# Threshold attention and an exact-gelu MLP in fp32: the first queries and keys loaded in longer rows, and the weights' conversion spread over ScalarE, GpSimd and SyncE

## The chip, the cores and the metric

The kernel runs on one core of a Trainium2 chip. A core has TensorE (PE) for matmuls, VectorE (DVE), ScalarE (ACT) and GpSimd (POOL) for elementwise work, SyncE (SP), which here only issues transfers, and 16 DMA engines. Operands lie in SBUF with 128 partitions, and matmuls write to PSUM. Each engine takes its instructions in the order of the program; engines wait for one another by semaphores. The metric is the device time of one execution in microseconds (us).

## The reference

```python
# q, k, v: (8 batches, 8 heads, 576 rows, 64);  tau = 0.02
scores = (1 / sqrt(64)) * q @ k.T
thresh = max(scores, axis=-1) - tau
scores = where(scores >= thresh, scores, -1e9)
attn = exp(scores - max(scores))
attn = attn / (sum(attn) + 1e-9)
x = (attn @ v), heads side by side        # (4608, 512)
h = x @ w_in                              # w_in (512, 2048)
g = 0.5 * h * (1 + erf(h / sqrt(2)))
out = g @ w_out                           # w_out (2048, 512)
```

The weights w_in and w_out reach the kernel as 64-bit floats. It converts them to 32 bits on the chip.

## The kernel before

**Work units.** Two heads of one batch form a pair; there are 32 pairs (NP), four to a batch (HP). The 576 query rows of a pair are cut in five chunks: four of 128 rows for each head and one in which the 64 last rows of both heads are joined (chunk NC = 4). One pair and one chunk make a slot. In a slot TensorE computes the scores (L348), VectorE their negated maxima (nmx, L360), GpSimd the threshold (thr, L361), ScalarE the exp (L363), and VectorE masks the exp by the threshold and sums it (L379).

**Order of slots.** The four pairs of the first batch are called early (EARLY = 4). Slots 0 to 7 take chunks 0 and 1 of these pairs, slots 8 to 19 chunks 2, 3 and 4; from slot 20 on (BATCH) pairs come one by one with all their chunks. All instructions are written out in program order in one loop over slots (n), and nothing reorders them. So an engine that waits keeps everything behind that instruction waiting.

**Early pairs.** Their q and k are loaded by `load_early` with a row of the sequence on a partition, and turned on TensorE by `turn_qk_early` (L265, tails L273), with ScalarE copying the result to SBUF. Keys may be in any order, so k's rows are taken four to a partition, in rows of 256 bytes of memory each per head; v's early load uses the same order. The masked exp is turned on TensorE against a diagonal matrix that holds the reciprocal of the sums: GpSimd adds 1e-9 to the sums (den, L382), VectorE takes the reciprocal (L390), ScalarE makes the diagonals (diag, L393), and a slot later `turn_p_early` turns (L291) and ScalarE copies to pT (L299, L302, L309, L314). `weigh_v` multiplies pT by v (xT, L465), and ScalarE copies the product to x (L470). For later pairs VectorE and DMAs turn p, and the division comes at the end, on GpSimd (L484).

**Weights.** There are 32 pieces of 128 x 512, 16 of w_in and then 16 of w_out. `load_piece` loads the raw 8-byte words of one piece (raw, L146) and, from three bytes further on, the same words again (shifted, L148): 1 MB for a piece. Four pieces can be in flight; even ones lie in two x tiles and odd ones in the two halves of turned_p. The first two are issued by SyncE before the loop; all others are issued by GpSimd, one of them whenever a piece has been converted. The generator `conversions` emits a piece's steps: VectorE masks the exponent (power, L168), ScalarE rebiases it (L169), VectorE takes the mantissa's bits (L174), puts the sign on the power (L176) and multiplies mantissa and power (L178). L168 of the next piece goes ahead of L174 of this one. `convert` emits steps in each slot until a budget in ns (the sum of the `yield` values) is used up: 0 in slot 0, 3400 in slots 1 to 7, 3650 in slots 8 to 18 and all that is left in slot 19. The call stands behind the masked sum of its slot and ahead of `diagonal`, so VectorE takes the reciprocal after the conversion of that slot.

**MLP.** A block is 256 tokens. `block_steps` yields its matmuls one at a time (hT, L536, then o_ps, L550), and `fill` places them between the slots' other work, when a piece that they need has been converted earlier in program order. From slot 20 on, `gelus_held` runs the first gelus, whose inputs were kept so that ScalarE needn't change its function table earlier, and `table` changes the table back. The last blocks are multiplied in `strassen` (L670), after all slots.

**Transfers.** SyncE issues the early loads, in the order of the program: q, k and v of pairs 0 to 3 (k of pair 0 by ScalarE, k of pair 1 by GpSimd) ahead of the slots that use them, then q, k and v of pairs 4 and 5 (`load`, L214 and L223), at the last chunks of pairs 1 and 2. GpSimd issues those of later pairs.

Of the kernel before, what the change touches and what calls it, by code (L numbers as in the profile page):

```python
# [8 lines left out]
FP32 = mybir.dt.float32  # L9
# [9 lines left out]
def kernel(  # L19
# [33 lines left out]
    P = 128  # L53
# [72 lines left out]
    loaded = [0]  # L126
    converted = [0]

    def load_piece(eng=nc.gpsimd):
        if loaded[0] == len(pieces):  # L130
            return
        dst, src = pieces[loaded[0]]
        loaded[0] += 1
        if not wide:
            nc.sync.dma_start(dst, src)
            converted[0] += 1
            load_piece()
            return
        k = loaded[0] - 1
        if k % 2:  # L140

            room = pd[k // 2 % 2].bitcast(U32)
            raw, shifted = room[:, 0:2 * PIECE], room[:, 2 * PIECE:4 * PIECE]
        else:
            raw, shifted = (xg.tile([P, 2 * PIECE], U32, tag="x", name=s) for s in ("raw", "shifted"))
        eng.dma_start(raw, src.bitcast(U32))  # L146
        n = 8 * PIECE - 4
        eng.dma_start(shifted.bitcast(U8)[:, 0:n], src.bitcast(U8)[:, 3:3 + n])  # L148
        raws.append((dst, raw, shifted))

    def conversions():

        vec = nc.vector
        ahead = None  # L160
        while raws or ahead:
            piece = None
            if raws:
                dst, raw, shifted = raws.pop(0)
                hi = raw.rearrange("p (f w) -> p f w", w=2)[:, :, 1]
                top = shifted.rearrange("p (f w) -> p f w", w=2)[:, :, 0]
                power = gp.tile([P, PIECE], U32, tag="g", name="power")
                vec.tensor_scalar(power, hi, 0x7FF00000, None, op0=ALU.bitwise_and)  # L168
                nc.scalar.activation(power, power, AF.Relu, bias=rebias, scale=8.0)  # L169
                piece = dst, hi, top, dst.bitcast(U32), power  # L170
                yield 340
            if ahead:
                dst, hi, top, mant, power = ahead
                vec.tensor_scalar(mant, top, 0x0FFFFFFF, 0x10000000, op0=ALU.bitwise_and, op1=ALU.bitwise_or)  # L174
                yield 340
                vec.scalar_tensor_tensor(power, hi, 0x80000000, power, op0=ALU.bitwise_and, op1=ALU.bitwise_or)  # L176
                yield 720
                vec.scalar_tensor_tensor(dst, mant, 2.0 ** -28, power.bitcast(FP32), op0=ALU.mult, op1=ALU.mult)  # L178
                load_piece()
                converted[0] += 1  # L180
                yield 700
            ahead = piece

    conv = {"steps": None, "debt": 0.0}
# [1 line left out]
    def convert(ns):  # L186

        if conv["steps"] is None:
            conv["steps"] = conversions()
        conv["debt"] += ns  # L190
        while conv["debt"] > 0:
            took = next(conv["steps"], None)
            if took is None:
                return
            conv["debt"] -= took
# [31 lines left out]
    def load_early(p):  # L227
        b, hp = divmod(p, HP)
        s = st[p] = {}
        for name, src in (("q", q), ("k", k)):  # L230
            t = s[name] = ld.tile([P, NC + 1, P], FP32, tag=name, name=name)
            eng = (nc.scalar, nc.gpsimd)[p] if p < 2 and name == "k" else nc.sync
            for e in range(2):
                order = "(t p) d -> p t d" if name == "q" else "(p t) d -> p t d"
                eng.dma_start(
                    t[:, 0:NC, e * D:(e + 1) * D], src[b, 2 * hp + e, 0:MAIN, :].rearrange(order, p=P))
            eng.dma_start(
                t[0:TAIL, NC, :].rearrange("p (e d) -> p e d", e=2),
                src[b, 2 * hp:2 * hp + 2, MAIN:S, :].rearrange("e s d -> s e d"),
            )  # L240

    def load_v_early(p):
        b, hp = divmod(p, HP)
# [5 lines left out]
    def turn_qk_early(p):  # L249


        s = st[p]
        if 2 <= p < HP:
            qT = op.tile([P, MAIN], FP32, tag="o_sb", name="qT")
            kT = pd_tail[p - 2].rearrange("p b i -> p (b i)")
        else:
            qT = ld.tile([P, MAIN], FP32, tag="qT", name="qT")
            kT = ld.tile([P, TAIL + S], FP32, tag="kT", name="kT")
        s["qT"], s["kT"] = qT, kT
        qt = s["q_tail"] = q_tail[p % 4]  # L260
        for name in "qk":
            t = s[name]
            tr = ps.tile([P, NC, P], FP32, tag="mm", name="tr")
            for c in range(NC):
                nc.tensor.transpose(tr[:, c, :], t[:, c, :], ident)  # L265
            src = tr.rearrange("p c s -> p (c s)")
            if name == "q":
                nc.scalar.activation(qT, src, AF.Copy, bias=0.0, scale=q_scale)
            else:
                nc.scalar.copy(kT[:, TAIL:S], src)  # L270
        tr = ps.tile([P, NC, P], FP32, tag="mm", name="tr")
        for j, name in enumerate("qk"):
            nc.tensor.transpose(tr[:, j, 0:TAIL], s.pop(name)[0:TAIL, NC, :], ident[0:TAIL, 0:TAIL])  # L273
        nc.scalar.copy(kT[:, S:S + TAIL], tr[:, 1, 0:TAIL])
        nc.scalar.copy(kT[D:P, 0:TAIL], tr[D:P, 1, 0:TAIL])
        for e in range(2):
            rows = slice(e * D, (e + 1) * D)
            nc.scalar.activation(
                qt[rows, e * TAIL:(e + 1) * TAIL], tr[rows, 0, 0:TAIL], AF.Copy, bias=0.0, scale=q_scale[rows])

    def turn_p_early(p, i):


        s = st[p]
        if i == 0 or (p < HP and i == 2):
            s["pT"] = [one.tile([P, KR, S], FP32, tag=f"pT{e}", name=f"pT{e}") for e in range(2)]
        w, diag = s.pop(("p", i)), s.pop(("diag", i))
        n = 1 if i == NC else 2

        def turn(to, cols, e):  # L290
            nc.tensor.matmul(to, lhsT=w[:, cols], rhs=diag[:, e, :], start=True, stop=True)  # L291

        for e in range(n):
            tr = ps.tile([P, NC, P], FP32, tag="mm", name="tr")
            for c in range(NC):
                at = e * (S + TAIL) + c * P
                turn(tr[:, c, :], slice(at, at + P), e)
            if i < NC:
                nc.scalar.copy(s["pT"][e][:, 0:NC, i * P:(i + 1) * P], tr)  # L299
        if i == NC:  # L300
            for e in range(2):
                nc.scalar.copy(s["pT"][e][:, 0:NC, MAIN:S], tr[:, :, e * TAIL:(e + 1) * TAIL])  # L302
        tails = s["pT"][0][:, NC, :]
        tr = ps.tile([P, NC, P], FP32, tag="mm", name="tr")
        if i < NC:
            for e in range(2):
                at = MAIN + e * TAIL
                turn(tr[e * TAIL:(e + 1) * TAIL, 0, :], slice(at, at + TAIL), e)
            nc.scalar.copy(tails[:, i * P:(i + 1) * P], tr[:, 0, :])  # L309
            return  # L310
        turn(tr[0:TAIL, 0, :], slice(MAIN, S), 0)
        for e in range(2):
            rows = slice(e * TAIL, (e + 1) * TAIL)
            nc.scalar.copy(tails[rows, MAIN:S], tr[0:TAIL, 0, rows])  # L314

    def scale_q(p):
        t = st[p]["q"]
# [132 lines left out]
    def weigh_v(p, lo, hi):  # L450


        b, hp = divmod(p, HP)
        s = st[p]
        xT = ps.tile([P, 512], FP32, tag="mm", name="xT")
        for c in range(KR):
            for e in range(2):
                f = slice(e * D, (e + 1) * D)
                to = xT[f, 0:hi - lo]
                if p < EARLY:  # L460
                    rhs = s["pT"][0 if c == NC else e][:, c, lo:hi]
                else:
                    to = to.rearrange("p (g s) -> p g s", s=2 * Q)
                    rhs = by_64(s["pT"][e])[:, lo // (2 * Q):hi // (2 * Q), c, :]
                nc.tensor.matmul(  # L465
                    to, lhsT=s["v"][:, e, c, :], rhs=rhs, start=(c == 0), stop=(c == KR - 1))
        for n, o, at, size in in_blocks(b, lo, hi):
            if n not in x_blk:
                x_blk[n] = xg.tile([P, N_DM, TOK], FP32, tag="x", name="x")
            nc.scalar.copy(x_blk[n][:, hp, o:o + size], xT[:, at - lo:at - lo + size])  # L470

    def in_blocks(b, lo, hi):
        while lo < hi:
# [311 lines left out]
    for t in q_tail + v_sb:  # L785
        nc.gpsimd.memset(t, 0.0)
    for _ in range(2):
        load_piece(nc.sync)
    turn_qk_early(0)
    load_v_early(0)  # L790
    load_early(2)
# [31 lines left out]
    for n in range(len(slots) + WEIGH + 1):  # L823
# [60 lines left out]
            scale_q(p + 1)  # L884
        if p >= HP - 1 and i == 2 and p + 1 < NP:
            turn_qk(p + 1)
        convert(0 if n == 0 else 3400 if n < 2 * HP else 3650 if n < BATCH - 1 else 1e9)
        if early:
            diagonal(p, i)
        if not early:  # L890
# [51 lines left out]
```

## Time and profile before

Three runs took 1392.73, 1394.04 and 1394.57 us. The profiled execution spans 1393.5 us.

| what | value |
|---|---|
| TensorE busy | 1360.1 us, 98% |
| VectorE busy | 891.4 us, 64% |
| ScalarE busy | 640.4 us, 46% |
| GpSimd busy | 433.4 us, 31% |
| VectorE's conversion, 10 to 150 us: L168, L174, L176, L178 | 435, 415, 684, 691 ns each |
| ScalarE's rebias L169 | 724 ns each |
| GpSimd's issue of one raw load | 0.55 to 0.6 us |
| SyncE's issue of one raw load | 0.35 to 0.43 us |

In groups of instructions a name left of the arrow is what is written, one to the right what is read. "Idle before" is time in which the engine had nothing running ahead of that instruction, and the name behind it is what the engine then waited for. A line with "SPq" or "POOLq" shows the issue of a transfer by SyncE or GpSimd, not its length. The granted clock is TensorE's, as a share of its full speed.

### The profile page before, as it was taken

What the parts mean: (1) busy time and instruction counts of PE and PEld (TensorE: products, weight loads), DVE (VectorE), ACT (ScalarE), POOL (GpSimd) and SP (SyncE); (2) the same over time, 40 slices, a digit from 0 to 9 for tenths busy, and PEclk for the clock granted to TensorE, in tenths of its full rate; (3) what the DMA queues carried; (4) which work ended last, traced back from release to release, by engine and by line L of the source; (5) the groups of instructions that cost most, each with busy time, mean ns of one, the idle gap of its engine ahead of it and who ended that gap; (6) DMA issues with size and microseconds to landing.
All of it is one profiled execution on the core that took longest, in us unless ns stands there. A gap on an engine that the chain in (4) does not pass through costs nothing.

```text
span 1393.5 us, 19980 instructions
## 1 busy us (share of the span) xinstructions
PE 1360.1 (98%) x6608; PEld 967.6 (69%) x6608; DVE 891.4 (64%) x1734; ACT 640.4 (46%) x1165; POOL 433.4 (31%) x895
## 2 busy tenths in 40 slices
PE   6799899999999999999999999999999999999999
PEld 4577547557457467466466476588888888888887
DVE  5889687788888888888888888764132242241330
ACT  5666636547447457457457357241141240330420
POOL 4444254455455455555554551100000000000000
PEclk9899999999999999999999999999999999999999
DMA  9889267667777777777778776500000001001000
GB/s 271 251 299 287 52 132 168 145 151 160 176 164 169 168 181 179 163 190 184 159 192 187 152 178 141 118 1 8 23 1 23 23 1 46 16 0 53 9 8 23
DMA packets 219557, 169.18 MB, mean 121 GB/s; under 512 B 121456, under 2 KB 203952, under 8 KB 219456
## 3 DMA queue, kind: packets, MB, share of 16 engines
q1 hardware_dynamic: 194768, 112.84, 36.2%
q0 software_dynamic: 23488, 54.77, 12.9%
q8 instruction: 54, 0.88, 0.3%
q10 hardware_dynamic: 1200, 0.30, 0.1%
q14 instruction: 47, 0.39, 0.1%
HBM read 72.73 MB, written 12.52 MB: 61 GB/s over the span
## 4 chain that ended last, share of the span: by engine, by line
PE 88%; DVE 5%; DMA 3%; ACT 3%; issue 1%; SPq 0%; POOL 0%; ACTq 0%; DVEq 0%
PE bank L670 35%; PE o_ps L550 16%; PE hT L536 14%; PE sc L348 12%; PE xT L465 10%; DVE p L379 1%; DVE power L176 1%; ACT p L363 1%; DMA k<-in_k_dram 1%; ACT diag L393 1%; DVE power L168 1%; DVE w_in L178 1%; DMA turned_p<-in_moe_w_in_dram 1%; DMA turned_p<-in_moe_w_out_dram 1%; DVE w_out L178 1%
## 5 line engine op out<-in xcount | busy, mean ns | idle before, releaser
L363 ACT ACTIVATE p<-sc,nmx 128x576 f32<-128x576 f32 x288 | 201.9, 738 | 271.5 <-DVE nmx L360 271.5
L379 DVE SCALAR_TENSOR_TENSOR p<-sc,thr,p 128x576 f32<-128x576 f32 x288 | 225.4, 816 | 70.0 <-ACT p L363 68.9
L360 DVE TENSOR_REDUCE nmx<-sc 128x1 f32<-128x576 f32 x288 | 205.3, 750 | 69.4 <-PE sc L348 68.6
L536 PE MATMUL hT<-x,w_in 128*128 128x256 f32 x1024 | 241.1, 385 | 0.0
L550 PE MATMUL o_ps<-w_out,g 128*128 128x512 f32 x512 | 237.3, 604 | 2.1 <-ACT pT L302 2.1
L536 PEld LDWEIGHTS hT<-x,w_in 128*128 128x128 f32 x1024 | 189.5, 190 | 49.2 <-issue 23.5
L361 POOL TENSOR_SCALAR thr<-nmx,tau_eff 128x1 f32<-128x1 f32 x288 | 84.4, 293 | 395.9 <-DVE nmx L360 395.1
L550 PEld LDWEIGHTS o_ps<-w_out,g 128*128 128x128 f32 x512 | 92.9, 189 | 112.7 <-issue 108.6
L465 PE MATMUL xT<-pT,v 128*64 128x256 f32 (+1 forms) x1280 | 163.9, 409 | 0.6 <-issue 0.6
L348 PE MATMUL sc<-kT,qT 64*128 64x288 f32 x960 | 158.5, 433 | 3.4 <-DVE p L379 2.5
L426 DVE STREAM_TRANSPOSE turned_p<-p 128x1152 f32<-128x1152 f32 x112 | 154.4, 1378 | 3.9
L348 PEld LDWEIGHTS sc<-kT,qT 64*128 64x128 f32 x960 | 90.3, 188 | 77.2 <-issue 64.8
L465 PEld LDWEIGHTS xT<-pT,v 128*64 128x64 f32 x1280 | 89.0, 137 | 73.2 <-issue 13.9
L670 PE MATMUL bank<-x,w_in 128*128 128x256 f32 x480 | 116.7, 379 | 0.0
L670 PE MATMUL bank<-w_out,unit 128*128 128x256 f32 x520 | 115.5, 379 | 0.0
L223 POOL DMA_DIRECT2D v<-in_v_dram x208 | 111.1, 537 | 4.6 <-issue 2.6
L670 PEld LDWEIGHTS bank<-w_out,unit 128*128 128x128 f32 x520 | 98.8, 190 | 13.4
L670 PEld LDWEIGHTS bank<-x,w_in 128*128 128x128 f32 x480 | 91.2, 190 | 12.8 <-issue 0.5
L670 PE MATMUL bank<-v,unit 128*128 128x256 f32 x320 | 82.1, 379 | 0.0
L214 POOL DMA_DIRECT2D q<-in_q_dram x104 | 70.9, 687 | 10.0 <-issue 9.1
L670 PE MATMUL bank<-unit,turned_p 128*128 128x256 f32 x320 | 73.1, 379 | 0.0
L509 ACT ACT_TABLE_LOAD x56 | 71.8, 1283 | 1.0
(154 smaller groups left out, 1487.6 us busy)
## 6 DMA issues: line engine op xcount, KB each, us to landing
pT<-turned_p SPq DMA_DIRECT2D x448, 160.0 KB, 3.7
pT<-pd_tail SPq DMA_DIRECT2D x112, 80.0 KB, 3.1
q<-in_q_dram POOLq DMA_DIRECT2D x104, 72.0 KB, 3.4
k<-in_k_dram POOLq DMA_DIRECT2D x104, 72.0 KB, 3.0
inv<-turned SPq DMA_DIRECT2D x56, 128.0 KB, 4.0
v<-in_v_dram POOLq DMA_DIRECT2D x156, 40.0 KB, 3.2
x<-x SPq DMA_DIRECT2D x10, 512.0 KB, 4.8
raw<-in_moe_w_out_dram POOLq DMA_DIRECT2D x8, 512.0 KB, 5.4
```

Of the source, the lines that this page charges most:

```text
L223: eng.dma_start(t[r:P:4, e, 0:n, :], rows[:, r * KR:r * KR + n, :])
L348: nc.tensor.matmul(sc[e][:, h, 0:HALF], lhsT=lhsT, rhs=s["kT"][rows, at:at + HALF], start=True, stop=True)
L360: nc.vector.tensor_reduce(nmx[:, e:e + 1], sc, axis=AXIS.XY, op=ALU.max, negate=True)
L361: nc.gpsimd.tensor_scalar(thr[:, e:e + 1], nmx[:, e:e + 1], -1.0, tau_eff, op0=ALU.mult, op1=ALU.subtract)
L363: nc.scalar.activation(w[:, e * S:(e + 1) * S].rearrange("p (h s) -> p h s", h=2), sc, AF.Exp, bias=nmx[:, e:e + 1], scale=1.0)
L379: nc.vector.scalar_tensor_tensor(row, sc[e][:, :, 0:HALF], thr[:, e:e + 1], row, op0=ALU.is_ge, op1=ALU.mult, accum_out=den[e])
L426: nc.vector.transpose(turned_p[:, :, i // 2, 0:NB, i % 2 * Q:(i % 2 + 1) * Q], w.rearrange("p (e b i) -> p e b i", e=2, i=Q))
L465: nc.tensor.matmul(to, lhsT=s["v"][:, e, c, :], rhs=rhs, start=(c == 0), stop=(c == KR - 1))
L509: nc.scalar.activation(t, src, AF.Gelu)
L536: nc.tensor.matmul(hT[:, j % 2, :], lhsT=w_in_sb[c][:, j * P:(j + 1) * P], rhs=x_blk[n][:, c, :], start=(c == 0), stop=(c == N_DM - 1))
L550: nc.tensor.matmul(o[:, 0:d_model], lhsT=g[j][:, m * P:(m + 1) * P], rhs=w_out_sb[j], start=(j == 0), stop=(j == N_DF - 1))
L670: nc.tensor.matmul(to, lhsT=l, rhs=r, start=start and k == 0, stop=k == len(pairs) - 1, skip_group_check=not start)
```

## The change

Four edits go together.

1. Early q and k are laid out with the head ahead of the chunk, so that a partition takes rows that lie next to each other in memory: two rows of q (512 bytes) and four of k (1 KB) at a time. Each turn of 128 columns becomes two matmuls of 64 columns, one for each head. The rows of q then come in another order within 256 tokens, which `weigh_v` puts right as it copies to x.
2. The product of mantissa and power leaves VectorE: ScalarE makes the mantissa a float and scales it, and GpSimd multiplies it by the power. `load_piece` for the piece four further on is now called after L176. The budgets of `convert` are 2000 in slots 1 and 2 and 2600 up to slot 18.
3. SyncE issues all raw weights.
4. For the last early pair (p = 3), VectorE copies the turned tails of p in place of ScalarE. This happens in slot 20.

```diff
-    def load_piece(eng=nc.gpsimd):
+    def load_piece(eng=nc.sync):
...
                 vec.scalar_tensor_tensor(power, hi, 0x80000000, power, op0=ALU.bitwise_and, op1=ALU.bitwise_or)
+                load_piece()
+                nc.scalar.activation(dst, mant, AF.Copy, bias=0.0, scale=2.0 ** -28)
+                nc.gpsimd.tensor_tensor(dst, dst, power.bitcast(FP32), op=ALU.mult)
+                converted[0] += 1
                 yield 720
-                vec.scalar_tensor_tensor(dst, mant, 2.0 ** -28, power.bitcast(FP32), op0=ALU.mult, op1=ALU.mult)
-                load_piece()
-                converted[0] += 1
-                yield 700
...
-            t = s[name] = ld.tile([P, NC + 1, P], FP32, tag=name, name=name)
+            t = s[name] = ld.tile([P, 2, NC + 1, D], FP32, tag=name, name=name)
...
+                rows = src[b, 2 * hp + e, 0:MAIN, :]
+                if name == "q":
+                    eng.dma_start(t[:, e, 0:NC, :].rearrange("p (g c) d -> p g (c d)", c=2),
+                                  rows.rearrange("(g p c) d -> p g (c d)", p=P, c=2))
+                else:
+                    eng.dma_start(t[:, e, 0:NC, :], rows.rearrange("(p t) d -> p t d", p=P))
...
-                nc.tensor.transpose(tr[:, c, :], t[:, c, :], ident)
+                for e in range(2):
+                    nc.tensor.matmul(tr[e * D:(e + 1) * D, c, :], lhsT=t[:, e, c, :], rhs=ident, start=True, stop=True)
...
+            copy = nc.vector.tensor_copy if p == EARLY - 1 else nc.scalar.copy
             for e in range(2):
-                nc.scalar.copy(s["pT"][e][:, 0:NC, MAIN:S], tr[:, :, e * TAIL:(e + 1) * TAIL])
+                copy(s["pT"][e][:, 0:NC, MAIN:S], tr[:, :, e * TAIL:(e + 1) * TAIL])
...
-        convert(0 if n == 0 else 3400 if n < 2 * HP else 3650 if n < BATCH - 1 else 1e9)
+        convert(0 if n == 0 else 2000 if n < 3 else 2600 if n < BATCH - 1 else 1e9)
```

More of the change, by code (lines that the diff above doesn't have):

```diff
@@ L230, in load_early @@
         for name, src in (("q", q), ("k", k)):
-            t = s[name] = ld.tile([P, NC + 1, P], FP32, tag=name, name=name)
+            t = s[name] = ld.tile([P, 2, NC + 1, D], FP32, tag=name, name=name)
             eng = (nc.scalar, nc.gpsimd)[p] if p < 2 and name == "k" else nc.sync
             for e in range(2):
[L234 to L240, printed above, removed]
+                rows = src[b, 2 * hp + e, 0:MAIN, :]
[4 more added lines that the diff above has]
+                    eng.dma_start(t[:, e, 0:NC, :], rows.rearrange("(p t) d -> p t d", p=P))
+            eng.dma_start(t[0:TAIL, :, NC, :], src[b, 2 * hp:2 * hp + 2, MAIN:S, :].rearrange("e s d -> s e d"))
     def load_v_early(p):
@@ L272, in turn_qk_early @@
         for j, name in enumerate("qk"):
-            nc.tensor.transpose(tr[:, j, 0:TAIL], s.pop(name)[0:TAIL, NC, :], ident[0:TAIL, 0:TAIL])
+            t = s.pop(name)
+            for e in range(2):
+                nc.tensor.matmul(tr[e * D:(e + 1) * D, j, 0:TAIL], lhsT=t[0:TAIL, e, NC, :],
+                                 rhs=ident[0:TAIL, 0:TAIL], start=True, stop=True)
         nc.scalar.copy(kT[:, S:S + TAIL], tr[:, 1, 0:TAIL])
@@ L313, in turn_p_early @@
             rows = slice(e * TAIL, (e + 1) * TAIL)
-            nc.scalar.copy(tails[rows, MAIN:S], tr[0:TAIL, 0, rows])
+            copy(tails[rows, MAIN:S], tr[0:TAIL, 0, rows])
     def scale_q(p):
@@ L469, in weigh_v @@
                 x_blk[n] = xg.tile([P, N_DM, TOK], FP32, tag="x", name="x")
-            nc.scalar.copy(x_blk[n][:, hp, o:o + size], xT[:, at - lo:at - lo + size])
+            to, x = x_blk[n][:, hp, o:o + size], xT[:, at - lo:at - lo + size]
+            if p < EARLY and size == TOK:
+                to = to.rearrange("q (p c) -> q c p", c=2)
+                x = x.rearrange("q (c p) -> q c p", c=2)
+            nc.scalar.copy(to, x)
     def in_blocks(b, lo, hi):
@@ L787 @@
     for _ in range(2):
-        load_piece(nc.sync)
+        load_piece()
     turn_qk_early(0)
```

## The prediction

> **What bounds the kernel now.** I read first which engine is busy in which stretch of the trace, because a change that touches only the first 32 weight pieces can move only the stretch in which they are converted. Columns: stretch, its length, busy us of TensorE (PE), its weight loads, VectorE (DVE), ScalarE (ACT), GpSimd (POOL), granted clock, DMA share, GB/s.
>
> ```profile
> 8.00:82.00 74.00, 59.42 (x381) 45.65 (x382) 58.97 (x129) 50.22 (x108) 30.76 (x62) 0.88 0.93 279
> 82.00:150.00 68.00, 64.98 (x401) 49.00 (x399) 60.33 (x133) 44.43 (x97) 27.95 (x56) 1.00 0.75 250
> 150.00:175.00 25.00, 21.03 (x88) 11.52 (x88) 12.23 (x21) 16.13 (x28) 7.29 (x20) 0.93 0.29 62
> 175.00:900.00 725.00, 724.26 (x3486) 433.53 (x3484) 607.38 (x1085) 400.15 (x608) 359.66 (x738) 1.00 0.73 165
> 900.00:1393.00 493.00, 487.85 (x2248) 426.22 (x2246) 151.71 (x362) 127.14 (x323) 1.69 (x3) 1.00 0.05 18
> ```
>
> After 175 us TensorE is busy 724 of 725 us and then 488 of 493; the change removes no TensorE work there, so nothing is to be had. Before it, TensorE idles 14.6 + 3.0 + 4.0 us, and its clock is 0.88 up to 82 us. So at stake are some 20 us at the start. The table of waits to 175 us says what TensorE waits for, and one line what the conversion waits for:
>
> ```profile
> PEld tr L291 <- ACT diag L393: 18.9, 10, 3.5
> ...
> PE tr L291 <- ACT diag L393: 14.4, 6, 3.1
> ...
> DVE power L168 <- DMA raw<-in_moe_w_in_dram: 4.6, 1, 4.6
> ...
> PE o_ps L550 <- ACT pT L302: 2.1, 1, 2.1
> ```
>
> The diag of a slot follows the reciprocal of its denominators (L390), which stands on VectorE behind that slot's conversion. VectorE is thus the bound up to 82 us: the reciprocals end at 14.27 us (slot 0), 21.81, 32.62, 40.13 and, for slot 9, 82.23. Slots 10 to 19 end at 149.53, 6.73 us each. VectorE's groups from 10 to 150 us (busy us, mean ns) give the conversion's price:
>
> ```profile
> L178 DVE SCALAR_TENSOR_TENSOR w_in<-w_in,power 128x512 f32<-128x512 uint32 x16 | 11.1, 691 | 0.4
> L178 DVE SCALAR_TENSOR_TENSOR w_out<-w_out,power 128x512 f32<-128x512 uint32 x16 | 11.1, 691 | 0.4
> L176 DVE SCALAR_TENSOR_TENSOR power<-raw,power 128x512 uint32<-128x512 uint32 x16 | 10.9, 684 | 0.1
> ```
>
> **What the Trainium skill says.** (1) "SBUF — State Buffer", section "Who interferes with whom": VectorE and GpSimd share a port pair under an exclusive lock; a VectorE operation with two SBUF inputs, or in a 2-port mode, and a GpSimd operation that reads SBUF block each other, while a tensor_reduce doesn't contend. The trace agrees as far as it goes: GpSimd's small add on the denominators (L382) takes 0.24 us at 14 us, and 0.62 and 0.89 us at 18 and 25 us, where conversion operations run on VectorE. (2) "GPSIMD Engine Reference", section "3.1 Elementwise — side-by-side cycle accounting": about 2.6 cycles an element on GpSimd, against 1 on VectorE. The trace's own slope serves instead (below). (3) "DMA: Bandwidth & Descriptors", section "Issuing engines are not separate DMA queues": all issuers use the same 16 DMA engines, another issuer saves only its own issue time. No run here shows it yet. (4) "TensorE: Matmul & The Clock Gate", section "What's actually happening": after an idle window of about 3.4 us the clock is halved until it is busy as long. The trace agrees: 20 turns (L291) take 2.42 us, and 3.9 to 4.4 us after idle.
>
> **The change part by part.**
> *VectorE loses L178.* 32 times; back to back they stand 0.61 us apart, so 32 × 0.61 = 19.6 us of VectorE's time. A slot with two pieces has about 3.2 us of softmax and 3.3 us of conversion. It falls to about 5.4; I take 5.7, since diag and exp on ScalarE now queue behind the new activations.
> *ScalarE gains 32 activations* of 128x512. The rebias (L169) of that shape takes 724 ns: 32 × 0.72 = 23 us. With 50.2 busy of 74 us and 44.4 of 68 there is room, so it costs only the 0.2 to 0.3 us a slot just named.
> *GpSimd gains 32 multiplies.* Its two-input multiply (L484) takes 729 ns for 256 columns and 457 for 128: 2.1 ns a column, so 729 + 256 × 2.1 = 1.27 us for 512, in all 41 us. It loses 60 issues of raw weights (L146, L148, 0.55 to 0.6 us each: 34 us). Its busy time hardly moves. Who waits? The threshold (L361) behind a multiply, which is needed only after the exp; and VectorE, if the lock holds it. Bounds of the lock: nothing, to one multiply of 1.2 us per slot where two pieces follow each other. I take nothing for the sum and keep the other end.
> *SyncE gains those 60 issues* (0.35 to 0.43 us each there), but in its own order. Before, GpSimd issued piece 2 at 14.29 us and VectorE took it up at 20.54. Now it stands behind SyncE's 28 loads of early q, k and v, which run from 10.78 to 32.40 us:
>
> ```profile
> 31.28 0.61 SPq L246 DMA_DIRECT2D v<-in_v_dram  x1
> 31.93 0.47 SPq L247 DMA_DIRECT2D v<-in_v_dram  x1
> 32.50 7.68 SPq L214 DMA_DIRECT2D q<-in_q_dram  x4
> ```
>
> Their waits are 2 us and more in places and shrink with the shorter lists of rows, so I take 28 us (bounds 24 and 32). Plus 4.6 us to land: 32.6. VectorE, in order, waits at slot 1's third L168 from 20.5 on: 12 us, and slot 1's reciprocal, its diag and the turns on TensorE stand behind it. The 4.6 us wait for piece 4 (28 to 32 us) goes: +7.5 us. Later the 16 loads of pair 4 (L214, L223: 11 to 20 us of SyncE) stand ahead of pieces 25 to 30, and those of pair 5 ahead of 31: up to 3 us in slots 14 to 17; I take 2.
> *Rows of 512 bytes and 1 KB.* Instead of 8192 rows of 256 bytes, 2048 of 512 and 1024 of 1 KB; the first q and k come somewhat sooner. In exchange each turn of 128 columns becomes two matmuls of 64. 16 turns take 4.0 us for q, 3.1 for k. The two halves use different columns, as the matmuls of xT do (20 records of 256 wide in 2.38 us, half the cost each of hT's). I take +0.6 us a head pair, 2.5 in all, bounds 0 and 7 (serial). Slot 0 +0.3, the rest under slot 1's wait.
> *Last tails on VectorE.* At slot 20 ScalarE switches tables, runs 6 gelus, switches back at 156.32, and only then copies the tails of p:
>
> ```profile
> 156.32 1.28 ACT L522 ACT_TABLE_LOAD   x1
> 157.62 0.20 ACT L522 ACTIVATE warm<-warm 128x1 f32<-128x1 f32 x1
> 157.72 0.63 ACT L302 COPY pT<-tr 128x256 f32<-128x256 f32 x2
> 158.24 0.42 ACT L314 COPY pT<-tr 64x64 f32<-64x64 f32 x2
> 158.41 1.63 PE L550 MATMUL o_ps<-w_out,g 128*128 128x512 f32 x2 [2.14 <-ACT pT L302]
> ```
>
> VectorE is free after the transpose that ends at 154.2 and would copy by about 155.2. The 2.14 us wait goes, and with it the half clock of the next 8 score matmuls (2.29 us, 8 × 0.14 warm = 1.1) and of the rest: about 1.8 more. −4 us; bounds −2 and −4. The copies' order of x (c before p) is the same number of elements in the same instruction: nothing.
>
> The sum. Up to slot 9: +7.5 for the wait, +2.5 for turns of which 2 lie under it, −8 slots × 0.8 (6.5 to 5.7) = −6.4, and about +1.5 for ends that TensorE's cold clock won't let it follow: +3. Slots 10 to 19: VectorE's 5.7 is below TensorE's need. TensorE's operations from slot 10's scores to slot 20's sum to 62.4 us back to back, against 68.5 taken; of the 6.1 some 2 stay as waits for diag and 2 go to SyncE's late pieces; where both fall on one slot they overlap, so I count 3 lost and **3 gained**. Slot 20: −4. Together +3 − 3 − 4 = **−4 us: 1394 − 4 = 1390**.
>
> **The rivals.**
> *B, slower, about 1400.* Lock and late pieces. The lock at its upper bound makes a slot 5.7 + 1.2 = 6.9 us: the 6.4 us of slots 2 to 9 become a loss of 3, slots 10 to 19 gain nothing (+1 to +2). Against −4 at slot 20 stand 7.5 + 2 + 3 + 2 = 14.5: up to +10, at two thirds of the lock +6. For it: L382's 0.89 us; against: the second multiply of a slot falls on the maxima (tensor_reduce) and the exp.
> *C, no change, about 1394.* The wait of slot 1 is 14 rather than 12 us, or TensorE keeps 4 us more of cold clock before 82 us; the gain of slot 20 is just paid. For it: TensorE is at 0.88 in this stretch and gets a longer idle time at slot 1.
> *D, larger gain, about 1384.* SyncE reaches piece 2 at 24 us: +3.5 in place of +7.5; slots 10 to 19 give 5 of their 6.1: −1 − 5 − 4 = −10. For it: nothing but the first of the bounds; against: SyncE's waits, seen in before.
>
> **How the numbers follow.** The forecast (a gain of 3 to 7 us) 0.43, D 0.13, C 0.14, B 0.30. 0.2% is 2.8 us. Faster is the forecast and D, 0.56; the same is C, 0.14; slower is B, 0.30. The range leaves out half of D and the worst third of B: 1384 to 1401.
>
> **What would show it.** Right: no L178 group on VectorE, reciprocals from slot 2 on nearer than 6 us to each other, a single long wait of L168 for raw weights at slot 1 (about 12 us, slot 1 ending near 32), slot 9 ending at 83 to 87 us, slot 19 near 149.5, no wait of o_ps for pT at slot 20. The lock shows as L168, L174 and L176 above their 435, 415 and 684 ns, or the multiply above 1.3 us. The forecast is wrong if slot 1's wait is much under or over 12 us, if VectorE's operations stretch, or if the late pieces cost waits of L168 in slots 14 to 17 beyond 2 us.

## The result, and the profile after

The changed kernel takes 1414.18 us (median; 1413.52 to 1415.2), the kernel before 1393.43 on the same chip: 1.0149 times as long, with a 95% interval of 1.0131 to 1.0166. It is 20.75 us slower, where 4 us less were forecast.

The same stretches of the changed kernel's trace (columns as before) show that the loss lies ahead of about 200 us; slot 20's reciprocal ends at 204.1 us in place of 185.2, and that is 19 of the 20 us by which the two traces differ:

```profile
8.00:82.00 74.00, 50.53 (x413) 38.74 (x413) 45.41 (x98) 50.28 (x108) 24.96 (x38) 0.85 0.76 247
82.00:150.00 68.00, 61.36 (x368) 46.31 (x367) 48.54 (x104) 48.77 (x105) 33.24 (x43) 0.93 0.82 263
150.00:175.00 25.00, 20.48 (x116) 15.20 (x117) 13.50 (x33) 13.51 (x29) 7.32 (x17) 0.93 0.18 54
175.00:900.00 725.00, 722.62 (x3481) 433.53 (x3482) 601.00 (x1074) 410.05 (x623) 362.65 (x743) 1.00 0.72 163
```

TensorE is busy 9 us less up to 82 us than before, and VectorE 45 us there where it was 59. VectorE has less to do and is idle more: it waits. TensorE's granted clock is 0.93 from 82 to 150 us, where it was 1.00. The changed kernel's table of waits up to 200 us (in total, times, longest) says for what. The line numbers have moved: L295 was L291, L384 was L379, L366 was L361.

```profile
POOL w_out L179 <- ACT w_out L178: 23.1, 9, 7.0
...
DVE power L168 <- DMA raw<-in_moe_w_in_dram: 13.8, 1, 13.8
DVE p L384 <- POOL thr L366: 13.7, 12, 2.4
...
DVE power L168 <- DMA turned_p<-in_moe_w_out_dram: 10.7, 2, 6.6
```

Three things are new: one long wait for raw weights, two later ones (10.7 us together), and a wait of the masked sum (L384) for GpSimd's threshold. The first two follow from SyncE's queue, shown here at its two places:

```profile
27.97 0.47 SPq L247 DMA_DIRECT2D v<-in_v_dram  x1
28.49 0.58 SPq L146 DMA_DIRECT2D raw<-in_moe_w_in_dram  x1
...
111.52 5.12 SPq L214 DMA_DIRECT2D q<-in_q_dram  x4
116.74 4.22 SPq L214 DMA_DIRECT2D k<-in_k_dram  x4
121.06 5.68 SPq L223 DMA_DIRECT2D v<-in_v_dram  x8
126.84 0.53 SPq L146 DMA_DIRECT2D turned_p<-in_moe_w_out_dram  x1
```

Piece 2 is issued at 28.49 us, behind the last early v. In the kernel before, GpSimd issued it at 14.29:

```profile
14.29 0.63 POOL L146 DMA_DIRECT2D raw<-in_moe_w_in_dram  x1
```

The loads of pair 4 take SyncE from 111.5 to 126.8 us, and the weights behind them come later. VectorE's lines that wait for these two, and for the first piece behind pair 5:

```profile
33.13 0.43 DVE L168 TENSOR_SCALAR power<-raw 128x512 uint32<-128x512 uint32 x1 [13.80 <-DMA raw<-in_moe_w_in_dram]
...
130.47 0.43 DVE L168 TENSOR_SCALAR power<-turned_p 128x512 uint32<-128x512 uint32 x1 [6.62 <-DMA turned_p<-in_moe_w_out_dram]
...
158.03 0.43 DVE L168 TENSOR_SCALAR power<-turned_p 128x512 uint32<-128x512 uint32 x1 [4.05 <-DMA turned_p<-in_moe_w_out_dram]
```

The ends of the reciprocals (start plus length in the timelines), which close a slot, in us. The times that the prediction calls ends are the starts, 0.15 us earlier. The table also has kernels of the next section. The two columns of differences are the time from slot 1 to slot 9, and from 9 to 19; the raw waits in them are VectorE's waits in L168.

| kernel | slot 1 | slot 9 | slot 19 | 1 to 9 | 9 to 19 |
|---|---|---|---|---|---|
| before | 21.96 | 82.38 | 149.68 | 60.4 (4.6 raw wait) | 67.3 |
| after | 33.64 | 93.40 | 170.23 | 59.8 | 76.8 (10.7 raw waits) |
| SyncE alone | 34.47 | 92.27 | 169.87 | 57.8 | 77.6 |
| split alone | 20.37 | 87.51 | 163.45 | 67.1 | 75.9 |
| after, no multiply | 34.32 | 88.85 | 163.49 | 54.5 | 74.6 |
| after, issue shared | 21.35 | 82.83 | 148.40 | 61.5 | 65.6 |

So slot 1 loses 11.7 us, slots 2 to 9 give only 0.7 back, and slots 10 to 19 lose 9.5 more. TensorE pays for a long wait once more, with a slower clock. Behind the wait of slot 1 its 20 turns (L295) take 4.41 us, and at 45 us 2.42:

```profile
34.66 4.41 PE L295 MATMUL tr<-diag,p 128*128 128x128 f32 x20 [15.79 <-ACT diag L398]
...
45.00 2.42 PE L295 MATMUL tr<-diag,p 128*128 128x128 f32 x20
```

Behind the wait of slot 14 they take 4.35 us; the granted clock from 132 to 136 us is 0.50.

In slot 20 the wait of o_ps for pT is gone, as forecast; VectorE has copied before the matmul comes:

```profile
176.84 0.72 DVE L307 COPY pT<-tr 128x256 f32<-128x256 f32 x2
177.48 0.43 DVE L319 COPY pT<-tr 64x64 f32<-64x64 f32 x2
178.07 1.02 PE L559 MATMUL o_ps<-w_out,g 128*128 128x512 f32 x2
```

### The profile page after: what moved, and what is told of

It reads as the page before. It is cut to its first block, busy times and chain, and to the rows that moved or that the text cites. A ratio compares the mean times of both kernels' runs of the same rounds, so it can differ in the third digit from the quotient of the medians.

```text
span 1413.4 us, 20304 instructions
## 1 busy us (share of the span) xinstructions
PE 1366.2 (97%) x6728; PEld 972.8 (69%) x6728; DVE 878.5 (62%) x1706; ACT 654.7 (46%) x1193; POOL 438.0 (31%) x867
## 4 chain that ended last, share of the span: by engine, by line
PE 88%; DVE 5%; ACT 2%; SPq 2%; DMA 1%; issue 1%; POOL 1%; DVEq 0%; ACTq 0%; POOLq 0%
PE bank L679 34%; PE o_ps L559 15%; PE hT L545 15%; PE sc L353 12%; PE xT L470 10%; PE tr L295 1%; DVE p L384 1%; DVE power L176 1%; ACT p L368 1%; DVE power L168 1%; DVE nmx L365 1%; SPq L223 1%; DMA turned_p<-in_moe_w_out_dram 1%; SPq L214 0%; ACT diag L398 0%
## 5 line engine op out<-in xcount | busy, mean ns | idle before, releaser
L384 DVE SCALAR_TENSOR_TENSOR p<-sc,thr,p 128x576 f32<-128x576 f32 x288 | 225.3, 815 | 78.3 <-ACT p L368 63.4
L366 POOL TENSOR_SCALAR thr<-nmx,tau_eff 128x1 f32<-128x1 f32 x288 | 84.1, 293 | 383.1 <-DVE nmx L365 382.3
L353 PEld LDWEIGHTS sc<-kT,qT 64*128 64x128 f32 x960 | 89.3, 186 | 74.6 <-issue 63.2
L295 PE MATMUL tr<-diag,p 128*128 128x128 f32 (+1 forms) x360 | 52.0, 317 | 33.7 <-ACT diag L398 24.1
L295 PEld LDWEIGHTS tr<-diag,p 128*128 128x128 f32 (+1 forms) x360 | 44.4, 206 | 43.2 <-ACT diag L398 29.3
L214 POOL DMA_DIRECT2D q<-in_q_dram x104 | 70.8, 686 | 8.5 <-issue 8.5
```

The source lines that it names most:

```text
L353: nc.tensor.matmul(sc[e][:, h, 0:HALF], lhsT=lhsT, rhs=s["kT"][rows, at:at + HALF], start=True, stop=True)
L366: nc.gpsimd.tensor_scalar(thr[:, e:e + 1], nmx[:, e:e + 1], -1.0, tau_eff, op0=ALU.mult, op1=ALU.subtract)
L384: nc.vector.scalar_tensor_tensor(row, sc[e][:, :, 0:HALF], thr[:, e:e + 1], row, op0=ALU.is_ge, op1=ALU.mult, accum_out=den[e])
```

## The experiments

Each was timed against the kernel before on the same chip (medians 1394.0 to 1394.9 us). A measured time stands with its ratio to the kernel before and the 95% interval of that ratio. "Less" and "more" without another name mean against the changed kernel's 1414.18 us, which was timed apart from these runs; such differences are good to 1 or 2 us. Theory S: SyncE's order makes the loss. Its rivals: M, the multiply standing in GpSimd's and ScalarE's queues, and L, the lock of the port that VectorE and GpSimd share.

**One part alone, on the kernel before.**

*SyncE alone.*
```diff
-    def load_piece(eng=nc.gpsimd):
+    def load_piece(eng=nc.sync):
```

> The kernel before, with one edit: SyncE issues all raw weights. Theory S (the order of SyncE's queue makes the loss): the wait for piece 2 at slot 1 is 12 to 14 us as in the changed kernel, and pieces behind the loads of pairs 4 and 5 make waits of 4 to 7 us in slots 14 and 17; the kernel takes 1408 to 1415 us. Theory M (the moved product makes the loss: GpSimd's multiply ahead of the threshold, ScalarE's copies ahead of diag and exp): SyncE alone costs at most 8 us, 1394 to 1402.

Measured: 1414.1 us, ratio 1.0133 (1.0114 to 1.0152). Slot 1 waits 12.2 us for piece 2 and slot 14 6.6 us:

```profile
33.03 0.43 DVE L168 TENSOR_SCALAR power<-raw 128x512 uint32<-128x512 uint32 x1 [12.22 <-DMA raw<-in_moe_w_in_dram]
...
130.41 0.43 DVE L168 TENSOR_SCALAR power<-raw 128x512 uint32<-128x512 uint32 x1 [6.57 <-DMA raw<-in_moe_w_out_dram]
```

One word of the diff alone gives the whole size of the loss: theory S is enough by itself.

*The split alone*, with GpSimd still issuing the weights. The diff is the one in `conversions` and in the call of `convert`.

> The kernel before, with one edit: the product is split over ScalarE and GpSimd with the new budgets; GpSimd still issues the raw weights. Theory S: VectorE's lighter slots show, 1385 to 1392 us. Theory M: the masked sum waits for the threshold (some 14 us in all) as in the changed kernel, slots 2 to 9 are no shorter than before, and the time is 1395 to 1406 us.

Measured: 1412.53 us, 1.0116 (1.0096 to 1.0136): more than either theory. So the split is a second, separate way to lose as much, when GpSimd both issues and multiplies; it is busy 47.0 of 74 us here up to 82 us, and 25.0 in the changed kernel. The masked sum's wait for the threshold, from this kernel's table up to 200 us:

```profile
DVE p L379 <- POOL thr L361: 30.2, 16, 3.7
```

In the changed kernel this wait was 13.7 us. The lock shows too: VectorE's conversion takes 61.4 us in this kernel, against 49.3 for the same operations before (L168 on raw 743 ns, against 435). How the 18 us divide between the wait and the lock, no run here shows. The two losses don't add up (19 and 18 apart, 21 together with a gain of 4 from the tails): in the changed kernel GpSimd no longer issues, and both losses fall on the same slots.

*Rows alone.* The diff is that of `load_early`, `turn_qk_early` and `weigh_v`.

> The kernel before, with one edit: early q and k in rows of 512 bytes and 1 KB, turned by two matmuls of 64 columns. Both theories: 1392 to 1396 us; slot 0 ends within 0.6 us of before, and each pair's turns take 0.6 us more. If the shorter lists of rows let SyncE come to later loads earlier, and any slot waited for them, it would be below 1391.

Measured: 1394.61 us, 0.9996 (0.9986 to 1.0007): no difference.

*Tails alone.* The diff is that of `turn_p_early`.

> The kernel before, with one edit: VectorE copies the turned tails of the last early pair in slot 20. Both theories: the 2.1 us wait of o_ps for pT goes and with it some half-clock matmuls: 1389.5 to 1392 us. If another wait takes its place (the scores or the gelus of slot 20), 1393 to 1394.

Measured: 1391.11 us, 0.9975 (0.9962 to 0.9989): 3.8 us less than before. From slot 19's reciprocal to slot 20's it takes 31.5 us, against 35.5 before. (One trace says little here: with the rows alone and the tails on ScalarE this took 33.9 us. The times carry the claim.)

**One suspect taken from the changed kernel.**

*Piece 2 ahead of the early loads.*
```diff
-    for _ in range(2):
+    for _ in range(3):
         load_piece()
...
-            if p < 2:
+            if p == 1:
                 load_piece()
```

> The changed kernel, with one edit: SyncE issues piece 2 ahead of the loop with pieces 0 and 1, ahead of the early loads (and none in slot 0). Theory S (the queue's order, and what it costs stays in the sum): the 13.8 us wait of slot 1 goes, slot 9 ends 8 to 11 us earlier and the time falls by 7 to 11 us, to 1403 to 1407. Theory M (the split product paces the slots anyway): slot 1 ends 10 us earlier but slots 2 to 9 take some 66 us, as with the split product alone, and the time falls by no more than 4 us, to 1410 or more.

Measured: 1407.42 us, 1.0092 (1.0079 to 1.0105), 6.8 us less. Slot 1 ends at 21.76, but slot 2 at 37.26: VectorE now waits 9.6 us for piece 3, which stands where piece 2 stood. The time falls nearly as far as theory S has it. Slots 2 to 9 take 65.0 us, as M has it, but for another reason: the new wait lies in them.

*Loads of pairs 4 and 5 in steps.*
```diff
-        if p < HP and i == NC and 0 < p < HP - 1:
-            load(p + 3)
+        if n in LOADS:
+            next(ahead45[LOADS[n]], None)
...
+    LOADS = {9: 4, 10: 4, 11: 5, 12: 5, 13: 4, 14: 4, 16: 5, 17: 5}
+    ahead45 = {x: load_steps(x) for x in (4, 5)}
```

> The changed kernel, with one edit: SyncE's loads of pairs 4 and 5 come in single steps of 4 issues, spread over slots 9 to 17, and no longer 16 at once. Theory S: the waits of VectorE for raw weights of 6.6 and 4.1 us in slots 14 and 17 go, and the time falls by 8 to 10 us, to 1404 to 1406. Theory M: slots 14 to 19 are paced by ScalarE and GpSimd, and it falls by no more than 4 us.

Measured: 1407.1 us, 1.0092 (1.0079 to 1.0105), 7.1 us less. From slot 9 to slot 19 it takes 71.0 us in place of 76.8, and the two waits are gone; theory S had a little more (8 to 10).

*The products one slot later*, behind the exp and the threshold.
```diff
-                nc.scalar.activation(dst, mant, AF.Copy, bias=0.0, scale=2.0 ** -28)
-                nc.gpsimd.tensor_tensor(dst, dst, power.bitcast(FP32), op=ALU.mult)
-                converted[0] += 1
+                products.append((dst, mant, power))
...
             softmax_head(p, i)
+            multiply()
```

> The changed kernel, with one edit: the activation and the multiply of a piece are emitted in the next slot, behind that slot's exp on ScalarE and its threshold on GpSimd. TensorE's order is the same. Theory M: the wait of the masked sum for the threshold (13.7 us in all) goes, diag comes sooner, and the time falls by 5 to 10 us, to 1404 to 1409. Theory S (SyncE's two late loads decide): at most 3 us. Theory L (the port lock is what the split costs): VectorE's L168, L174 and L176 stretch as before or more, and the time stays within 3 us of 1414.

Measured: 1422.07 us, 1.0197 (1.0184 to 1.021): 8 us more. The wait for the threshold is down to 1.2 us, as M has it, and the kernel is slower, by more than any of the theories has. The timeline of this kernel shows the lock at work:

```profile
68.08 2.68 POOL L157 TENSOR_TENSOR w_in<-w_in,power 128x512 f32<-128x512 f32 x2 [1.42 <-ACT w_in L156]
...
68.43 1.20 DVE L183 TENSOR_SCALAR w_in<-shifted 128x512 uint32<-128x512 uint32 x1
...
69.55 1.75 DVE L185 SCALAR_TENSOR_TENSOR power<-raw,power 128x512 uint32<-128x512 uint32 x1
...
71.56 0.41 DVE L183 TENSOR_SCALAR w_in<-turned_p 128x512 uint32<-128x512 uint32 x1
```

While GpSimd's two multiplies run, the mantissa mask (L183, L174 above) takes 1.20 us and the sign (L185, L176 above) 1.75; the next mask, after the multiplies, takes 0.41. In this kernel the three conversion groups have 30.0, 20.5 and 23.9 us of VectorE's time, 74.4 together, against 49.3 for the same 96 operations before (21.8, 14.2, and 13.3 from 32 × 0.416): 25 us, more than the 22.2 us of L178 that the split takes off. Where the change itself puts the multiply, it falls mostly on the maxima, which it doesn't hold, and the lock costs some 7 us, from the groups of the changed kernel that are longer than 435, 415 and 684 ns:

```profile
L176 DVE SCALAR_TENSOR_TENSOR power<-turned_p,power 128x512 uint32<-128x512 uint32 x16 | 13.1, 821 | 0.1
...
L168 DVE TENSOR_SCALAR power<-raw 128x512 uint32<-128x512 uint32 x16 | 8.9, 558 | 13.8 <-DMA raw<-in_moe_w_in_dram 13.8
L168 DVE TENSOR_SCALAR power<-turned_p 128x512 uint32<-128x512 uint32 x16 | 7.8, 489 | 10.7 <-DMA turned_p<-in_moe_w_out_dram 10.7
L174 DVE TENSOR_SCALAR w_in<-turned_p 128x512 uint32<-128x512 uint32 x8 | 4.5, 557 | 0.0
L174 DVE TENSOR_SCALAR w_out<-turned_p 128x512 uint32<-128x512 uint32 x8 | 4.5, 556 | 0.0
```

But there it stands ahead of the threshold. Behind it, it holds the conversion. Neither of the two places is free.

*All three edits* (piece 2 ahead, loads in steps, products later).

> The changed kernel with all three edits. If the late raw pieces and the two queues' order are the whole loss, the lighter VectorE shows and the time is below the kernel before, 1384 to 1391 us. If the lock takes back what VectorE was given, 1392 to 1398 us. If ScalarE's 23 us more are a bound of their own, 1396 to 1402.

Measured: 1405.13 us, 1.0078 (1.0061 to 1.0095). Above all three expectations. The other two edits without the later products take 1397.8 us (below), so the later products spoil what these give.

*Thresholds on VectorE.*
```diff
-            nc.gpsimd.tensor_scalar(
+            (nc.vector if p < EARLY else nc.gpsimd).tensor_scalar(
                 thr[:, e:e + 1], nmx[:, e:e + 1], -1.0, tau_eff, op0=ALU.mult, op1=ALU.subtract)
```

> The changed kernel, with one edit: in the early slots the threshold is taken by VectorE, behind each maximum, and not by GpSimd. Theory M (the multiply costs by standing ahead of the threshold on GpSimd): the 13.7 us of waits of the masked sum go, two small operations a slot (some 0.2 us) come, and the time falls by 5 to 9 us. Theory L (what the multiply costs is the port lock): the multiply still holds L168, L174 and L176, and the time falls by less than 3 us. Theory S (SyncE's order alone): no change.

Measured: 1415.2 us, 1.0148 (1.0133 to 1.0163): no change. The 13.7 us of waits are gone, and slots 2 to 9 take 3.1 us less in the trace. Slots 14 and 17 wait for raw weights as before (10.5 us in all), slots 10 to 19 take 77.1 us in place of 76.8, and slot 20 still ends 1.8 us earlier. The times show nothing of it; where it goes isn't shown.

*Without the multiply.* GpSimd's multiply is left out, so the weights are the bare mantissas.

> The changed kernel without GpSimd's multiply: the product of mantissa and power is left out, so the weights are the bare mantissas; all else stays, SyncE's order with it. This gives the whole price of the multiply, lock and queue together. Theories M and L together: L168, L174 and L176 are back at 435, 415 and 684 ns, no wait for the threshold, and the time falls by 7 to 12 us, to 1402 to 1407. Theory S: at most 3 us.

Measured: 1407.16 us, 1.0089 (1.0074 to 1.0105): 7 us less. With SyncE's order the same in all, slots 2 to 9 take 57.8 us with the product on VectorE (SyncE alone, which has the shorter rows and ScalarE's tails), 59.8 with the split, 54.5 without the multiply: the lighter VectorE is worth 3.3 us there, and the multiply costs 5.3. This is what M and L have together, and theory S alone, with at most 3 us, doesn't account for it. VectorE's instructions and waits in slots 2 to 9, summed from the timelines (us), say where the lighter work goes:

| kernel | pieces | conversion | waits, raw weights apart | for the exp | for the threshold |
|---|---|---|---|---|---|
| before | 13 | 29.0 | 6.0 | 4.1 | 0 |
| after | 15 | 26.7 | 12.6 | 2.5 | 6.2 |
| after, no multiply | 15 | 22.6 | 11.8 | 7.7 | 0 |

The multiply stretches the conversion by 4.1 us, and the wait for the threshold stands where otherwise VectorE would wait for the exp. Even without the multiply most of VectorE's saving, 6.4 us with two pieces more, turns into waits for ScalarE and TensorE (5.8 us more than before).

*Both edits to SyncE's order.*

> The changed kernel with both edits to SyncE's order: piece 2 ahead of the early loads, and the loads of pairs 4 and 5 in steps of 4 issues. If the two late-piece waits are separate parts of the loss they add up (6.7 and 7.1 us): 1400 to 1401 us. What is then left above the kernel before without the split, some 6 to 7 us and the 3.8 of the tails, is the price of the split product. If fixing one makes the other worth less: 1403 to 1406.

Measured: 1397.8 us, 1.0027 (1.0015 to 1.0039): 16.4 us less than the changed kernel, a little more than the two alone together (6.8 and 7.1). One long wait, of 11.4 us for piece 3, is left.

*Pieces 0 to 3 ahead of the loop*, and the loads in steps; then with the product on VectorE; then with the thresholds on VectorE.

> The changed kernel with pieces 0 to 3 issued by SyncE ahead of the loop (none in slots 0 and 2) and the loads of pairs 4 and 5 in steps of 4 issues. With two pieces ahead of the early loads a wait of 11.4 us for piece 3 had taken the place of that for piece 2. Theory S: now no wait for raw weights is over 3 us, slot 2 ends near 28, and the time is 1390 to 1394. If the early q, k and v, now later, take its place: 1397 or more.

> The same order of SyncE as in the run beside it, with the product on VectorE and the old budgets: the difference of the two is the price of the split alone, with GpSimd issuing none of the weights in both. If the split costs by lock and queue what it saves on VectorE: within 2 us of the run beside it. If it costs more: 3 us and more below it, 1386 to 1390. If the lighter VectorE pays once the pieces are early: above it by 3 us or more.

> The first run with the early thresholds on VectorE as well. With SyncE's order out of the way the waits for the threshold (13 us) can count: if they are what is left of the multiply's price, it is 3 to 5 us below the first run; if the lock and ScalarE's queue are, within 2 us.

Measured: 1403.03 (1.0052; 1.0033 to 1.007), 1397.4 (1.0023; 1.0009 to 1.0036) and 1399.18 us (1.0037; 1.0026 to 1.0047). The cure that theory S had (1390 to 1394 us) failed. In the first, the wait has moved to pieces 4 and 5:

```profile
39.55 0.43 DVE L168 TENSOR_SCALAR power<-raw 128x512 uint32<-128x512 uint32 x1 [6.02 <-DMA raw<-in_moe_w_in_dram]
42.98 0.43 DVE L168 TENSOR_SCALAR power<-turned_p 128x512 uint32<-128x512 uint32 x1 [2.06 <-DMA turned_p<-in_moe_w_in_dram]
```

In each of the three orders tried so far (two, three and four pieces ahead) the next piece stands behind SyncE's early loads. Here the split takes 5.6 us more than the product on VectorE, although the latter has a wait of 10.0 us for raw weights in slot 2; the two intervals overlap at their ends.

*Issue shared.* GpSimd issues pieces 2 to 5 beside SyncE's early loads, SyncE all others; the loads of pairs 4 and 5 in steps. Again with the thresholds on VectorE, and with the product on VectorE.
```diff
+        eng = nc.gpsimd if 2 <= loaded[0] < 6 else nc.sync
```

> The changed kernel with pieces 2 to 5 issued by GpSimd, which stands beside SyncE's early loads, all later ones by SyncE, and the loads of pairs 4 and 5 in steps of 4 issues. Theory S in full (SyncE's order is all that the change loses): no wait for raw weights over 5 us, and 1388 to 1392 us. With the split's own price of 4 to 6 us: 1393 to 1397.

> The same with the early thresholds on VectorE. If the wait for the threshold behind the multiply is most of the split's price: 2 to 4 us below the run beside it; if lock and ScalarE's queue are: the same within 1.5 us.

> The same order of issue with the product on VectorE and the old budgets, so GpSimd issues less and multiplies nothing. The tails give their 3.8 us: 1389 to 1391.5. If GpSimd's issues of raw weights had delayed its thresholds and sums before, 1386 to 1388.

Measured: 1392.89 (0.9985; 0.9973 to 0.9997), 1392.44 (0.9974; 0.9959 to 0.9988) and 1395.1 us (1.0004; 0.9992 to 1.0016). In the first, VectorE's longest wait for raw weights is 1.29 us (L169 here is L168 of the changed kernel):

```profile
20.24 1.04 DVE L169 TENSOR_SCALAR power<-raw 128x512 uint32<-128x512 uint32 x1 [0.99 <-DMA raw<-in_moe_w_in_dram]
43.94 0.43 DVE L169 TENSOR_SCALAR power<-turned_p 128x512 uint32<-128x512 uint32 x1 [0.82 <-DMA turned_p<-in_moe_w_in_dram]
...
101.64 1.37 DVE L169 TENSOR_SCALAR power<-raw 128x512 uint32<-128x512 uint32 x1 [1.29 <-DMA raw<-in_moe_w_out_dram]
```

This undoes the whole loss, 21.3 us, with the split, the rows and the tails left in. Theory S holds for the loss of the changed kernel: SyncE's order makes it alone, and mending the order ends it. The product on VectorE in the same order isn't better: its slots 10 to 19 take 70.8 us, against 67.3 before, with waits for raw weights of up to 2.2 us, which may be where the tails' 4 us go. So the split as such no longer loses, but it doesn't win either: the kernel before with the tails alone is at 0.9975. The thresholds on VectorE take off 3.9 us with four pieces ahead, 0.4 with the issue shared and nothing in the changed kernel, so what the wait for the threshold costs stays open.

*The best version: tails, and earlier pieces on the kernel before.* The tails on VectorE; piece 2 issued by SyncE ahead of the loop, piece 3 in slot 0 and none in slot 2.

> The kernel before with VectorE's copies of the last tails, and with piece 2 issued by SyncE ahead of the loop, piece 3 in slot 0 and none in slot 2, so that piece 4 is issued by GpSimd behind the first piece's conversion in slot 1. The product stays on VectorE. The tails give 3.8 us. If the wait of 4.6 us for piece 4 in slot 2 goes and nothing takes its place: 1386 to 1388 us. If another wait takes its place: 1390 to 1391.

Measured: 1389.54 us, 0.9967 (0.9959 to 0.9975), 5.1 us less than before, the lowest median here. No wait of L168 is left at slots 1 to 3, but most of the gain is that of the tails: their interval alone reaches down to 0.9962, so it isn't shown that the earlier pieces add to it.

## Why the prediction was wrong

It had the parts right, and those that it took for small were the loss. Against its sum the traces are 8.0 us worse up to slot 9 (+11.0, where it has +3), 12.5 us worse in slots 10 to 19 (+9.5, where it has −3) and 2.4 us worse in slot 20.

- *"+7.5 us" for slot 1.* The mechanism and nearly all numbers held: issue at 28.49 us (28 taken), a wait of 13.8 (12 taken), end of slot 1 at 33.64 (near 32). But the 4.6 us of piece 4, which I took off at once, came off only in slots 2 to 9, where they were eaten; slot 1's 11.7 us were still 11.0 at slot 9. (Of the 28 loads that stand ahead of piece 2, the trace of before has 24 between 10.78 and 32.40 us; the first four start at 7.86 us. The sum took only the end.)
- *GpSimd, "I take nothing for the sum and keep the other end".* This step failed. The −6.4 us of slots 2 to 9 became −0.7, and that includes the 4.6 us of piece 4: some 10 us are missing. Without the multiply 5.3 of them come back, and 4.1 of these are the lock's stretching of the conversion. The rest is that VectorE stops being the bound: I gave ScalarE's longer queue 0.3 us a slot, but without the multiply VectorE waits 3.6 us more for the exp and 1.6 us more for the scores. I also took one number of pieces a slot (3.3 us of conversion is 1.6 pieces, not two), while the new budgets put 15 pieces where 13 were. With the issue shared raw weights cost only 0.8 us in slots 2 to 9, and still these take 61.5 us: this step failed by itself, apart from SyncE. I had judged the threshold "needed only after the exp", and this is so; but the multiply ahead of it itself waits for ScalarE's activation, which stands behind other work (23.1 us of waits of the w_out multiplies for it). And the lock took some 7 us of the 22.2 saved up to slot 19. Where the trace of before had L382 at 0.89 us, the lock was there to be priced at one multiply per conversion operation that meets it, not at nothing.
- *"Up to 3 us in slots 14 to 17; I take 2."* This step failed too, and it is the largest single miss: VectorE waited 10.7 us, 8.7 more than taken. The size of SyncE's block was right (11 to 20 us taken, 15.3 measured for pair 4). What was wrong is how much of it the pieces in flight cover: VectorE waited 6.6 us behind pair 4 and 4.1 us behind pair 5. With the loads in steps the kernel took 7.1 us less.
- *Slots 10 to 19, "3 gained".* They lost 9.5 us, 10.7 of it for raw weights; the rest did gain 1.2. With the weights in time (issue shared) they take 65.6 us against 67.3: there is a recovery, of 1.7 us, little over half of what I took.
- *Slot 20, −4 us.* Right where it can be seen alone (3.8 us less in time; 31.5 against 35.5 us in the traces). In the changed kernel's trace it is 33.9.
- *Rows, +0.5 us.* Right within the noise (1394.61 us, 0.9996).
- *The clock.* That it is halved after idle time holds, but the idle window of 3.4 us isn't what the trace of before shows: the 20 turns (L291) took 3.89 to 4.41 us after waits of 2.18 to 3.09 us, and 2.42 us after one of 2.72.

Rival B named the right causes, the lock and the late pieces, but at +6. What set it apart from the forecast was mostly the lock. The runs put SyncE's order first: 19 us alone, and 21 us when it is cured with the split left in. The multiply is worth 7 us while SyncE's order stands.

What stays open: the split takes 5.6 us more than the product on VectorE with four pieces ahead, and 2.2 us less with the issue shared. The intervals overlap slightly in both cases (0.9973 to 0.9997 and 0.9992 to 1.0016 in the second). Whether the sign really changes with the place of the raw waits, and why, isn't shown.

## What to carry to other kernels

An engine that issues transfers is a queue like any other: before moving loads to it, write down what it has already to issue ahead of them, and at which time the consumer asks. Work that is moved to GpSimd needs a place where VectorE runs operations that don't share the port, and where nothing small that others wait for stands behind it. Before counting what an engine saves as time, look for the wait that ends next: here it was the exp. When a moved load's wait is cured and the next piece waits in its place, try to part the queue between two engines; here that did what three orders of one queue had not done.

## What the runs showed of the hardware

The Trainium skill, "SBUF — State Buffer", section "Who interferes with whom", states that the engine that issues first gets the shared ports for the whole instruction and the other one blocks. The trace of the later products agrees: a mask of 0.42 us took 1.20 and a sign of 0.69 us took 1.75 beside multiplies of 1.3 us, while the maxima stayed at 0.74 to 0.75 us, and the masked sum, which reads one input from PSUM, at 0.82. A threshold of one column takes VectorE 0.21 us, and GpSimd 0.29.
